# Channel mixing behind attention in a written-out order, u's parts kept in DRAM, and a sixth of its weights converted earlier

## Chip, cores, metric

One core of a Trainium2 chip runs the whole program. The metric is the device time of one execution in microseconds (us), as the median of three runs.

## What is computed

Three layers stand in a row: attention (4 batches, 8 heads, 576 positions, head size 64) as the sum of a local and a four times coarser softmax attention, a token and channel mixer, and a second mixer with a rotation.

```
x  = attention(q, k, v)                      # 4 x 576 x 512
h  = relu(x^T w_tok1) w_tok2                 # token mixing, 576 -> 256 -> 576
u  = x + h^T
x  = u + relu(u w_ch1) w_ch2                 # channel mixing, 512 -> 1536 -> 512
t  = x w_theta
y  = w_tok_r (x cos t) + w_tok_i (x sin t)   # 576 x 576
u  = x + y
out = u + relu(u w_ch)
```

All matrix products behind attention are made from a high and a low part of each operand, in three products (high x high, high x low, low x high).

## The kernel before

**Weights.** They arrive as 64-bit floats, seen as integers. A block is 128 x 256 (or 288) numbers, and `weights` (L106) converts one: a load `raw`; on ScalarE (ACT) the low word `wf` (L119) and the high word's magnitude `ww` (L121); on GpSimd (POOL), or for some of the first 33 blocks on VectorE (DVE), a clamp (L122); on DVE four operations that build the number (L126, L134) and its scale (L137, L144); on ACT the high part (L145); on POOL the difference (L146); on POOL or DVE the low part (L147). 9 blocks are of token mixing, 48 of channel mixing, 8 of `w_theta`, 18 of `w_ri`, 8 of `w_ch`.

**Channel mixing.** `channel_mix` (L184) does one batch b and one half of the 1536 channels, and in it two halves of the 576 tokens (`th`). I call one (b, half, th) a tile; there are 16. A tile loads `ut` and splits it into `uh` and `ul` (ACT and DVE, L94 and L95). Its first product runs over six blocks `cb` of 12 matmuls into a PSUM bank `c`; ACT makes the relu's high part (L214) and DVE the low part (L215), both named g in the trace. The second product runs over four blocks `db` of 18 matmuls, and DVE adds each to `ut` (L228). The result goes to `xT` in DRAM. The first half of the channels leaves u + part in `xT`, the second half splits u again, loads `xT` into `ut` and adds to it.

**Order.** A scheduler with a timeline model of its own orders the instructions of each engine from program order and priorities. In attention the string `ORDER` gives the program order: L, F, T, P, V are steps of local heads, coarse heads, token mixing and loads; `X` converts blocks of the first half's weights (24 in all), `C0` and `C1` do the first half of the channels for batches 0 and 1. Behind attention follow the first half for b = 2 and 3, then the second half for b = 0 to 3. Each tile is followed in program order by six conversions, `aside`: 24 blocks of the second half's weights, then 34 of the last layer (58 blocks over ten tiles). From there on `raw` is loaded on ACT's queue; all other loads and stores are on SP's.

Of the kernel before, what the change touches and what calls it, by code (L numbers as in the profile page):

```python
# [26 lines left out]

ORDER = """
# [3 lines left out]
T3 F5 T3 T3 L8 L8 T3 T3 P12 V10 L10 T3 T3 F5 L9 T3 T3 L9 F5 F5 L9 L9 T3 T3 P13 V11 C0 L11 L11 T4 F6 T4 F6 T4  # L32
T4 L10 L12 V12 P14 F6 T4 L10 L10 T4 T4 T4 T4 T4 F6 F6 L11 L11 T4 T4 P15 V13 L13 F7 F7 T5 T5 L12 T5 T5 L12 L12
T5 T5 V14 L14 F7 L13 L13 T5 T5 L13 F7 T5 T5 F7 T5 T5 V15 L15 C1 T6 T6 L14 L14 T6 L14 T6 T6 L15 L15 T6 L15 T6
T6 T6 T7 T7 T7 T7 T7 T7 T7 T7 T7 T6
""".split()
B, H, S, D = 4, 8, 576, 64
DM = H * D
# [21 lines left out]
def kernel(  # L60
# [23 lines left out]
    uT_d = [dram.tile([DM, S], F32, name=f"uT_{b}") for b in range(B)]  # L84
    xT_d = [dram.tile([DM, S], F32, name=f"xT_{b}") for b in range(B)]
# [18 lines left out]
    rawq = [nc.sync]  # L104

    def weights(stage, hi, lo, parts, adder=dve):  # L106

        n = hi.shape[-1]
        raw = stage.tile([128, n], parts[0][2].dtype, tag="raw", name="raw", bufs=4)
        for p0, p1, src in parts:  # L110
            rawq[0].dma_start(raw[p0:p1], src)
        if raw.dtype == I64:
            words = raw.bitcast(U32).rearrange("p (n t) -> p n t", t=2)
            high = raw.bitcast(F32).rearrange("p (n t) -> p n t", t=2)[:, :, 1]
            w = stage.tile([128, n], F32, tag="ww", name="ww")
            e = stage.tile([128, n], BF16, tag="we", name="we")
            f = stage.tile([128, n], BF16, tag="wf", name="wf")
# [6 lines left out]
            )  # L124
            wu = w.bitcast(U32)
# [10 lines left out]
            )  # L136
            dve.tensor_scalar(  # L137
# [6 lines left out]
            dve.tensor_tensor(out=f, in0=f, in1=e, op=ALU.mult)  # L144
            act.copy(hi, w)  # L145
            pool.tensor_tensor(out=w, in0=w, in1=hi.bitcast(F32), op=ALU.subtract)  # L146
            adder.tensor_tensor(out=lo, in0=w, in1=f, op=ALU.add)  # L147
        else:
            adder.tensor_copy(hi, raw)
            pool.tensor_tensor(out=lo, in0=raw, in1=hi.bitcast(F32), op=ALU.subtract)  # L150

    def load_split(pool_, stage, name, src, nk, n, chunk, adders=(pool, dve)):
# [4 lines left out]
        for c in range(0, n, chunk):  # L157
            for k in range(nk):
                def step(k=k, c=slice(c, c + chunk), adder=adders[len(steps) % len(adders)]):
                    weights(stage, hi[:, k, c], lo[:, k, c], [(0, 128, src[k * 128 : (k + 1) * 128, c])], adder)  # L160
                steps.append(step)
# [5 lines left out]
    hp = tc.alloc_tile_pool(name="hp", bufs=6)  # L167
    wlow = tc.alloc_tile_pool(name="wlow", bufs=1, side="right")
# [4 lines left out]
    def channel_weights(pool_, stage, half):  # L173
        c = slice(half * NCH, (half + 1) * NCH)
        adders = (pool, dve) if half else (pool,)
        h1, l1, s1 = load_split(pool_, stage, f"c1{half}", w_ch1[:, c], 4, NCH, 256, adders)
        h2, l2, s2 = load_split(pool_, stage, f"c2{half}", w_ch2[c, :], NCB, DM, 256, adders)
        return (h1, l1, h2, l2), s1 + s2
# [5 lines left out]
    def channel_mix(b, half, src, dst, w, mmb, queue, aside=(), per=0):  # L184

        w1h, w1l, w2h, w2l = w
        for th in range(2):
            t = slice(th * HALF, (th + 1) * HALF)
            at = f"{b}_{half}_{th}"
            here = half == 0 and b in DIRECT  # L190
# [12 lines left out]
            if half:  # L203
                queue.dma_start(ut, src[:, t].rearrange("(k p) n -> p k n", p=128))
            hs = []
            for cb in range(NCB):
                c = slice(cb * 128, (cb + 1) * 128)
# [11 lines left out]
            for db in range(4):  # L219
                d = slice(db * 128, (db + 1) * 128)  # L220
                ps = mmb.tile([128, 512], F32, tag="mb", name=f"c2_{at}_{db}")
                for cb in range(NCB):
                    pe.matmul(ps[:, 0:HALF], w2h[:, cb, d], hs[cb][0], start=(cb == 0), stop=False)  # L223
# [6 lines left out]
            for st in islice(aside, per):  # L230
                st()
# [608 lines left out]
```

## Time and profile before

| what | value |
|---|---|
| median of three runs | 787.59 us (784.44 to 788.61) |
| profiled execution: time, span | 786.98 us, 785.0 us |
| mean granted clock of TensorE | 0.959 of full speed |
| busy: TensorE (PE), DVE, ACT, POOL | 727.5, 478.5, 327.1, 263.6 us |
| moved by DMA | 91.33 MB |

The time is the device's own and holds a little work around the span. Busy time is the sum of an engine's instructions as recorded; matmuls overlap, so PE's is not its use. The clock is the share that was granted, 1.0 being 2.4 GHz and 0.5 being 1.2 GHz.

### The profile page before, as it was taken

The numbers are of one execution on the slowest core, as the hardware profiler recorded it, in microseconds if no ns is written. First come the engines' busy times: TensorE is split into PE (matmuls) and PEld (weight loads), VectorE is DVE, ScalarE is ACT, GpSimd is POOL, SyncE is SP. The second block draws the span as 40 slices with busy tenths as digits, with TensorE's granted clock in tenths as the row PEclk, the third lists the DMA queues.
The fourth block names the chain that finished last, engine by engine and source line by source line (L and its number), as shares of the span: only waits on it lengthen the run. The fifth ranks groups of instructions, "written<-read, shape, count | busy, mean of one in ns | idle before, by whom it ended". The sixth has DMA issues, their size and how long they took to land.

```text
span 785.0 us, 19821 instructions
## 1 busy us (share of the span) xinstructions
PE 727.5 (93%) x8272; PEld 684.1 (87%) x8272; DVE 478.5 (61%) x1007; ACT 327.1 (42%) x752; POOL 263.6 (34%) x276
## 2 busy tenths in 40 slices
PE   7687966899999999999898888999999999999998
PEld 4456755789988999899898888999999999999998
DVE  4998998545343332799899898423395366464432
ACT  2554645442243223455555554221384164253310
POOL 2688788422021000688788785000000000000000
PEclk9776969899999999999999999999999999999999
DMA  9566666257153213535656755231000400300101
GB/s 294 172 234 190 180 169 217 85 161 211 57 150 85 69 43 92 180 117 153 198 171 190 238 172 172 91 92 61 31 1 1 127 2 1 121 1 2 61 1 61
DMA packets 58314, 91.33 MB, mean 116 GB/s; under 512 B 7536, under 2 KB 38384, under 8 KB 58224
## 3 DMA queue, kind: packets, MB, share of 16 engines
q1 hardware_dynamic: 49872, 74.27, 30.7%
q10 hardware_dynamic: 8352, 15.80, 6.6%
q8 instruction: 65, 1.06, 0.6%
q14 instruction: 25, 0.20, 0.1%
HBM read 69.99 MB, written 20.05 MB: 115 GB/s over the span
## 4 chain that ended last, share of the span: by engine, by line
PE 56%; DVE 22%; issue 9%; POOL 6%; DMA 3%; ACT 3%; SPq 1%; ACTq 0%; POOLq 0%; DVEq 0%
PE y L98 5%; PE y L100 5%; PE y L99 5%; DVE ww L134 5%; DVE wf L144 4%; PE c L226 3%; PE c L98 3%; DVE we L137 3%; DVE ww L126 3%; PE c L223 3%; PE c L100 3%; PE c L99 3%; PE c L224 3%; POOL ww L122 3%; PE th L98 2%
## 5 line engine op out<-in xcount | busy, mean ns | idle before, releaser
L122 POOL TENSOR_SCALAR ww<-ww 128x256 f32<-128x256 f32 (+1 forms) x85 | 98.1, 1163 | 36.8 <-DVE ut L228 22.1
L215 DVE SCALAR_TENSOR_TENSOR g<-c,g 128x288 fp32r<-128x288 f32 x96 | 42.9, 450 | 62.3 <-ACT g L214 62.3
L100 PE MATMUL y<-wrh,zl 128*128 128x288 f32 x256 | 75.7, 296 | 0.0
L99 PE MATMUL y<-wrl,zh 128*128 128x288 f32 x256 | 75.6, 295 | 0.0
L98 PE MATMUL y<-wrh,zh 128*128 128x288 f32 x256 | 75.6, 296 | 0.0
L214 ACT ACTIVATE g<-c 128x288 fp32r<-128x288 f32 x96 | 38.7, 409 | 70.8 <-PE c L100 70.2
L496 POOL TENSOR_TENSOR x<-x,xu 128x640 f32<-128x640 f32 x16 | 25.3, 1591 | 106.7 <-DVE x L488 98.5
L223 PE MATMUL c<-g,c21h 128*128 128x288 f32 x192 | 53.4, 302 | 8.1 <-ACT g L214 8.1
L98 PE MATMUL c<-uh,c10h 128*128 128x288 f32 x192 | 58.2, 307 | 2.1 <-DVE ut L228 1.3
L100 PE MATMUL c<-uh,c10l 128*128 128x288 f32 x192 | 57.7, 301 | 0.0
L119 ACT ACTIVATE wf<-raw 128x256 bf16<-128x256 uint32 (+1 forms) x91 | 40.3, 443 | 41.3 <-DMA raw<-w_ch 7.8
L126 DVE TENSOR_SCALAR ww<-ww 128x256 uint32<-128x256 uint32 (+1 forms) x91 | 47.3, 521 | 16.6 <-POOL ww L122 14.8
L98 PE MATMUL c<-uh,c11h 128*128 128x288 f32 x192 | 56.9, 296 | 0.0
L99 PE MATMUL c<-ul,c10h 128*128 128x288 f32 x192 | 56.8, 296 | 0.0
L99 PE MATMUL c<-ul,c11h 128*128 128x288 f32 x192 | 56.7, 295 | 0.0
L100 PE MATMUL c<-uh,c11l 128*128 128x288 f32 x192 | 56.5, 294 | 0.0
L223 PE MATMUL c<-g,c20h 128*128 128x288 f32 x192 | 53.6, 303 | 1.6 <-ACT g L214 1.5
L224 PE MATMUL c<-g,c21l 128*128 128x288 f32 x192 | 53.1, 299 | 0.0
L224 PE MATMUL c<-g,c20l 128*128 128x288 f32 x192 | 52.2, 295 | 0.0
L134 DVE SCALAR_TENSOR_TENSOR ww<-raw,ww 128x256 uint32<-128x256 uint32 (+1 forms) x91 | 50.7, 559 | 1.0
L228 DVE TENSOR_TENSOR ut<-c,ut 128x288 f32<-128x288 f32 x56 | 25.2, 451 | 38.9 <-PE c L226 38.9
L99 PEld LDWEIGHTS y<-wrl,zh 128*128 128x128 f32 x256 | 48.1, 188 | 0.0
(190 smaller groups left out, 2274.5 us busy)
## 6 DMA issues: line engine op xcount, KB each, us to landing
qk<-qkT SPq DMA_DIRECT2D x16, 582.0 KB, 5.6
raw<-w_ch ACTq DMA_DIRECT2D x32, 256.0 KB, 2.9
ut<-uT SPq DMA_DIRECT2D x14, 576.0 KB, 4.1
xT<-ut SPq DMA_DIRECT2D x14, 576.0 KB, 3.1
vw<-vloc SPq DMA_DIRECT2D x32, 219.4 KB, 4.3
raw<-w_ch SPq DMA_DIRECT2D x24, 256.0 KB, 3.8
vd<-vtok SPq DMA_DIRECT2D x8, 650.0 KB, 6.6
raw<-w_ri ACTq DMA_DIRECT2D x18, 288.0 KB, 3.0
```

The source lines that it names most:

```text
L98: pe.matmul(out, lh, rh, start=start, stop=False)
L99: pe.matmul(out, lh, rl, start=False, stop=False)
L100: pe.matmul(out, ll, rh, start=False, stop=stop)
L119: act.activation(f, words[:, :, 0], AF.Copy, scale=2.0**-52)
L122: next(clamps).tensor_scalar(out=w, in0=w, scalar1=F64_LEAST, scalar2=F64_MOST, op0=ALU.max, op1=ALU.min)
L126: dve.tensor_scalar(out=wu, in0=wu, scalar1=3, scalar2=0x3FFFFFF8, op0=ALU.logical_shift_left, op1=ALU.bitwise_and,)
L134: dve.scalar_tensor_tensor(out=wu, in0=words[:, :, 1], scalar=0xC0000000, in1=wu, op0=ALU.bitwise_and, op1=ALU.bitwise_or)
L144: dve.tensor_tensor(out=f, in0=f, in1=e, op=ALU.mult)
L214: act.activation(h1, ps[:, 0:HALF], AF.Relu)
L215: dve.scalar_tensor_tensor(out=h2, in0=ps[:, 0:HALF], scalar=0.0, in1=h1.bitcast(F32), op0=ALU.max, op1=ALU.subtract)
L223: pe.matmul(ps[:, 0:HALF], w2h[:, cb, d], hs[cb][0], start=(cb == 0), stop=False)
L224: pe.matmul(ps[:, 0:HALF], w2l[:, cb, d], hs[cb][0], start=False, stop=False)
```

## The change

The weights of channel mixing are cut into six pieces of 256 channels instead of two halves. The fourth piece (8 blocks, named c13 and c23) is converted in attention by the new `Y` entries of `ORDER`, always with POOL for the clamp and the low part; 50 blocks stay behind attention. A conversion is now a generator (`converted`), which is advanced by half turns: load, four half turns later ACT and POOL's clamp, three later two operations of DVE, one later two more, three later ACT's high part and POOL's difference, three later the low part. A block starts at every second half turn, so some seven are under way.

Behind attention ACT, DVE, POOL and PE take program order (`manual_schedule`); SP's queue stays the scheduler's. `TURNS` gives the turns of each of the 12 tiles there, `SLOTS` the share of them that stands behind each of the ten evictions (six g, four additions). A tile's `ut` (and in the second half `uh` and `ul`) is loaded by `begin` a tile ahead; the split of the next `ut` stands, in quarters, behind the first two additions. In the first half `uh` and `ul` are stored to `parts_d`, and the second half loads them instead of splitting again. The second product takes the g of cb 0 to 3 first. `raw` stays on SP's queue.

```
-    rawq[0] = nc.scalar
+    depth[:] = 5, 6
...
-    for b in range(sum(e[0] == "C" for e in ORDER), B):
-        channel_mix(b, 0, None, xT_d[b], low, mmb if b == B - 2 else mmw, nc.sync, aside, 6)
...
+    def turn():
+        for g in list(live):
+            if next(g, "end") == "end":
+                live.remove(g)
+        g = next(blocks, lambda: None)() if next(halfturns) % 2 == 0 else None
+        if g is not None:
+            next(g)
+            live.append(g)
...
+    def begin(b, half, th):
...
+        nc.sync.dma_start(ut, src[:, t].rearrange("(k p) n -> p k n", p=128))
+        uh, ul = ((b3 if th else b1).tile([128, 4, HALF], F32R, tag=f"u{p}", name=f"u{p}_{at}") for p in "hl")
+        if half:
+            for t_, d_ in zip((uh, ul), parts_d[b][th]):
+                nc.sync.dma_start(t_.bitcast(F32), d_)
+            return (ut, uh, ul), []
+        steps = [partial(split, uh[:, kb, :], ul[:, kb, :], ut[:, kb, :]) for kb in range(4)]
+        return (ut, uh, ul), steps
...
+            for cbs in (range(4), range(4, NCB)):
+                for cb in cbs:
+                    w2h, w2l = w[cb // 2][2:4]
+                    pe.matmul(ps[:, 0:HALF], w2h[:, cb % 2, d], hs[cb][0], start=(cb == 0), stop=False)
+                    pe.matmul(ps[:, 0:HALF], w2l[:, cb % 2, d], hs[cb][0], start=False, stop=False)
+                for cb in cbs:
+                    last_one = cb == NCB - 1
+                    pe.matmul(ps[:, 0:HALF], w[cb // 2][2][:, cb % 2, d], hs[cb][1], start=False, stop=last_one)
...
+TURNS = [6, 6, 6, 5, 6, 6, 6, 6, 6, 6, 5, 0]
...
+    SLOTS = [0.08, 0.08, 0.08, 0.08, 0.02, 0.02, 0.16, 0.16, 0.16, 0.1601]
+    with tc.manual_schedule(engines={act.engine, dve.engine, pool.engine, pe.engine}):
+        loaded, steps = begin(*order[0])
...
+            def slot(i):
+                for _ in range(2 if NCB <= i < NCB + 2 else 0):
+                    next(rest, int)()
+                for _ in range(int(turns * sum(SLOTS[: i + 1])) - int(turns * sum(SLOTS[:i]))):
+                    turn()
+                next(side, int)()
+
+            mix(b, half, th, loaded, high if half else low, mmb if b == B - 2 and not half else mmw, slot)
```

In attention, DVE's queue of the kernel before reads as follows between the normalisation of a head pair (`ods`, `rl`, `x`) and the split of u (`ul`):

```order
L404 TENSOR_TENSOR ods_0_2429<-od_0_2397,rd_0_2426 128x320
L485 TENSOR_SCALAR rl_3_2484<-o_3_2443 128x10
L486 RECIPROCAL rl_3_2484<-rl_3_2484 128x10
L488 TENSOR_TENSOR x_1_2185<-o_3_2443,rl_3_2484 128x2x5x64
L215 SCALAR_TENSOR_TENSOR g_0_0_0_4_3002<-c_0_0_0_4_2988,g_0_0_0_4_3001 128x288
L215 SCALAR_TENSOR_TENSOR g_0_0_0_5_3019<-c_0_0_0_5_3005,g_0_0_0_5_3018 128x288
L95 TENSOR_TENSOR ul_0_1_3104<-um_1_1083,uh_0_1_3103 128x288 x3
```

At the same place the changed kernel has these (L136, L144, L149, L156 are the four operations of a conversion, L126, L134, L137, L144 before):

```order
L144 SCALAR_TENSOR_TENSOR ww<-raw,ww 128x256
L516 TENSOR_TENSOR x_1_2216<-o_3_2474,rl_3_2515 128x2x5x64
L149 TENSOR_SCALAR we<-ww 128x256
L136 TENSOR_SCALAR ww<-ww 128x256
L156 TENSOR_TENSOR wf<-wf,we 128x256
L144 SCALAR_TENSOR_TENSOR ww<-raw,ww 128x256
L239 SCALAR_TENSOR_TENSOR g_0_0_0_0_4_3035<-c_0_0_0_0_4_3021,g_0_0_0_0_4_3034 128x288
L149 TENSOR_SCALAR we<-ww 128x256
L156 TENSOR_TENSOR wf<-wf,we 128x256
L239 SCALAR_TENSOR_TENSOR g_0_0_0_0_5_3052<-c_0_0_0_0_5_3038,g_0_0_0_0_5_3051 128x288
L103 TENSOR_TENSOR ul_0_1_0_3137<-um_1_1114,uh_0_1_0_3136 128x288 x3
```

Conversions of the fourth piece now stand between `x`, the two g and the split; in all some 32 instructions were put between `h` of token mixing in batch 1, first half, and `h` of its second half. PE's order there stayed nearly as it was.

Behind attention, DVE's queue before has, around the end of the first product of b = 3 (g of cb 4 and 5, the next tile's split, the first addition):

```order
L215 SCALAR_TENSOR_TENSOR g_3_0_0_4_5506<-c_3_0_0_4_5492,g_3_0_0_4_5505 128x288
L137 TENSOR_SCALAR we<-ww 128x256
L147 TENSOR_TENSOR c21l<-ww,wf 128x256
L144 TENSOR_TENSOR wf<-wf,we 128x256
L215 SCALAR_TENSOR_TENSOR g_3_0_0_5_5523<-c_3_0_0_5_5509,g_3_0_0_5_5522 128x288
L126 TENSOR_SCALAR ww<-ww 128x256
L134 SCALAR_TENSOR_TENSOR ww<-raw,ww 128x256
L95 TENSOR_TENSOR ul_0_1_5700<-ut_0_1_5697,uh_0_1_5699 128x1152
L137 TENSOR_SCALAR we<-ww 128x256
L144 TENSOR_TENSOR wf<-wf,we 128x256
L126 TENSOR_SCALAR ww<-ww 128x256
L134 SCALAR_TENSOR_TENSOR ww<-raw,ww 128x256
L228 TENSOR_TENSOR ut_0_0_5418<-c_3_0_0_0_5526,ut_0_0_5418 128x288
```

and in the changed kernel:

```order
L709 SCALAR_TENSOR_TENSOR g_3_0_0_4_5683<-c_3_0_0_4_5669,g_3_0_0_4_5682 128x288
L136 TENSOR_SCALAR ww<-ww 128x256
L144 SCALAR_TENSOR_TENSOR ww<-raw,ww 128x256
L709 SCALAR_TENSOR_TENSOR g_3_0_0_5_5704<-c_3_0_0_5_5690,g_3_0_0_5_5703 128x288
L726 TENSOR_TENSOR ut_0_0_5283<-c_3_0_0_0_5707,ut_0_0_5283 128x288
L103 TENSOR_TENSOR ul_0_1_5572<-ut_0_1_5569,uh_0_1_5571 128x288 x2
L161 TENSOR_TENSOR c24l<-ww,wf 128x256
L149 TENSOR_SCALAR we<-ww 128x256
L156 TENSOR_TENSOR wf<-wf,we 128x256
L136 TENSOR_SCALAR ww<-ww 128x256
L144 SCALAR_TENSOR_TENSOR ww<-raw,ww 128x256
```

Nothing stands before the addition any more that isn't due; the conversions and two quarters of the split (x2) have moved behind it.

SP's queue of the kernel before has no `raw` behind attention; the changed one has, around the store of a finished tile (`xT`) and the loads of the next ones:

```order
L120 DMA raw<-w_ri 128x288
L688 DMA ul_1_1_6591<-ul_1_76 128x1152
L120 DMA raw<-w_ri 128x288
L688 DMA uh_1_1_6590<-uh_1_75 128x1152
L120 DMA raw<-w_ri 128x288 x3
L729 DMA xT_85<-ut_1_1_6075 128x4x288
L120 DMA raw<-w_ri 128x288
L684 DMA ut_1_1_6588<-xT_86 128x4x288
```

The loads of `ul` and `uh`, which wait for the first product of the tile that held their buffer, stand ahead of four of a tile's six raw loads.

## Rows read from the trace of the kernel before

**Rows 1.** The page, part 1: busy time, share of the span, instructions.

```profile
PE 727.5 (93%) x8272; PEld 684.1 (87%) x8272; DVE 478.5 (61%) x1007; ACT 327.1 (42%) x752; POOL 263.6 (34%) x276
```

**Rows 2.** The page, part 2: busy tenths in 40 slices; granted clock.

```profile
PE   7687966899999999999898888999999999999998
...
PEclk9776969899999999999999999999999999999999
```

**Rows 3.** Stretches: length; busy us (count) of PE, PEld, DVE, ACT, POOL; clock; DMA; GB/s.

```profile
142.39:166.79 24.40, 24.21 (x462) 21.91 (x463) 13.59 (x32) 10.52 (x28) 7.27 (x8) 0.94 0.45 134
168.00:297.00 129.00, 127.47 (x2172) 115.92 (x2172) 49.90 (x104) 39.22 (x91) 14.70 (x13) 1.00 0.35 105
296.94:558.00 261.06, 246.29 (x1812) 241.50 (x1810) 180.65 (x399) 114.53 (x276) 137.72 (x146) 0.99 0.46 143
320.00:480.00 160.00, 148.07 (x1082) 143.94 (x1081) 145.38 (x332) 87.38 (x221) 133.14 (x141) 1.00 0.56 173
500.00:558.00 58.00, 57.47 (x436) 57.24 (x434) 16.25 (x32) 11.63 (x24) 0.00 (x0) 1.00 0.22 67
```

**Rows 4.** Waits of PE from 315 to 500 us: total, times, longest us.

```profile
PE c L223 <- ACT g L214: 9.6, 10, 2.2
```

**Rows 5.** DVE groups, 320 to 480 us: busy us, mean ns, idle before.

```profile
L126 DVE TENSOR_SCALAR ww<-ww 128x256 uint32<-128x256 uint32 (+1 forms) x56 | 29.0, 518 | 7.8 <-POOL ww L122 6.4 <-DMA raw<-w_ch 1.1
L134 DVE SCALAR_TENSOR_TENSOR ww<-raw,ww 128x256 uint32<-128x256 uint32 (+1 forms) x56 | 28.2, 504 | 0.6
L144 DVE TENSOR_TENSOR wf<-wf,we 128x256 bf16<-128x256 bf16 (+1 forms) x56 | 28.0, 499 | 0.9
L137 DVE TENSOR_SCALAR we<-ww 128x256 uint16<-128x256 uint16 (+1 forms) x56 | 21.9, 391 | 0.5
L215 DVE SCALAR_TENSOR_TENSOR g<-c,g 128x288 fp32r<-128x288 f32 x43 | 19.2, 447 | 2.5 <-ACT g L214 2.5
L228 DVE TENSOR_TENSOR ut<-c,ut 128x288 f32<-128x288 f32 x30 | 13.3, 446 | 0.0
L95 DVE TENSOR_TENSOR ul<-ut,uh 128x1152 fp32r<-128x1152 f32 x7 | 9.7, 1379 | 0.0
...
L147 DVE TENSOR_TENSOR c21l<-ww,wf 128x256 fp32r<-128x256 f32 x6 | 3.7, 609 | 0.6 <-POOL ww L146 0.5
```

**Rows 6.** Groups by shape, whole span: u's split in quarters.

```profile
L95 DVE TENSOR_TENSOR ul<-um,uh 128x288 fp32r<-128x288 f32 x8 | 4.8, 618 | 0.3 <-ACT uh L94 0.3
```

**Rows 7.** The page, part 6: DMA issues, KB each, median us to landing.

```profile
raw<-w_ch ACTq DMA_DIRECT2D x32, 256.0 KB, 2.9
...
xT<-ut SPq DMA_DIRECT2D x14, 576.0 KB, 3.1
```

**Rows 8.** Two stretches of attention, columns as in rows 3.

```profile
136.00:140.00 4.00, 0.00 (x0) 0.10 (x1) 3.89 (x10) 2.33 (x8) 3.14 (x4) 0.82 0.51 208
140.00:144.00 4.00, 3.39 (x26) 2.56 (x26) 3.93 (x10) 3.13 (x10) 3.08 (x4) 0.50 0.02 4
```

**Rows 9.** Timeline of DVE: start us, length us, instruction, idle before.

```profile
110.92 0.42 DVE L134 SCALAR_TENSOR_TENSOR ww<-raw,ww 128x256 uint32<-128x256 uint32 x1
...
113.22 1.72 DVE L134 SCALAR_TENSOR_TENSOR ww<-raw,ww 128x256 uint32<-128x256 uint32 x1
...
141.97 0.42 DVE L521 SCALAR_TENSOR_TENSOR h<-t,h 128x256 fp32r<-128x256 f32 x1
...
166.79 0.42 DVE L521 SCALAR_TENSOR_TENSOR h<-t,h 128x256 fp32r<-128x256 f32 x1 [1.66 <-ACT h L520]
```

**Rows 10.** DVE groups by shape, 50 to 144.7 us.

```profile
L134 DVE SCALAR_TENSOR_TENSOR ww<-raw,ww 128x256 uint32<-128x256 uint32 x24 | 16.9, 706 | 0.2
L126 DVE TENSOR_SCALAR ww<-ww 128x256 uint32<-128x256 uint32 x24 | 13.3, 558 | 6.7 <-POOL ww L122 6.6
L144 DVE TENSOR_TENSOR wf<-wf,we 128x256 bf16<-128x256 bf16 x24 | 11.5, 485 | 0.4
L137 DVE TENSOR_SCALAR we<-ww 128x256 uint16<-128x256 uint16 x24 | 9.4, 398 | 0.2
```

More of the change, by code (lines that the diff above doesn't have):

```diff
@@ L2 @@
 from contextlib import ExitStack
-from itertools import chain, cycle, islice, repeat
+from functools import partial
+from itertools import chain, count, cycle, islice, repeat
 import numpy as np
@@ L84 @@
     uT_d = [dram.tile([DM, S], F32, name=f"uT_{b}") for b in range(B)]
+    parts_d = [
+        [[dram.tile([128, 4, HALF], F32, name=f"u{p}_{b}_{th}") for p in "hl"] for th in range(2)] for b in range(B)
+    ]
     xT_d = [dram.tile([DM, S], F32, name=f"xT_{b}") for b in range(B)]
@@ L103, with converted @@
     clamps = chain(islice(cycle([pool] * 4 + [dve]), 33), repeat(pool))
-    rawq = [nc.sync]
-    def weights(stage, hi, lo, parts, adder=dve):
+    rawq, depth = [nc.sync], [4, 3]
+    def converted(stage, hi, lo, parts, adder=dve):
         n = hi.shape[-1]
-        raw = stage.tile([128, n], parts[0][2].dtype, tag="raw", name="raw", bufs=4)
+        raw = stage.tile([128, n], parts[0][2].dtype, tag="raw", name="raw", bufs=depth[0])
         for p0, p1, src in parts:
             rawq[0].dma_start(raw[p0:p1], src)
+        yield from repeat(0, 4)
         if raw.dtype == I64:
@@ L136, in weights @@
             )
+            yield
+            e = stage.tile([128, n], BF16, tag="we", name="we", bufs=2)
             dve.tensor_scalar(
@@ L150, in weights @@
             pool.tensor_tensor(out=lo, in0=raw, in1=hi.bitcast(F32), op=ALU.subtract)
+    def weights(*args):
+        for _ in converted(*args):
+            pass
     def load_split(pool_, stage, name, src, nk, n, chunk, adders=(pool, dve)):
@@ L182, with channel_mix @@
     DIRECT = (0,)
-    def channel_mix(b, half, src, dst, w, mmb, queue, aside=(), per=0):
-        w1h, w1l, w2h, w2l = w
+    def channel_mix(b, half, src, dst, w, mmb, queue, cbs=range(NCB)):
         for th in range(2):
             t = slice(th * HALF, (th + 1) * HALF)
-            at = f"{b}_{half}_{th}"
-            here = half == 0 and b in DIRECT
+            at = f"{b}_{half}_{th}_{cbs[0]}"
+            here = src is None and b in DIRECT
             if here:
@@ new lines, with finish @@
+    live, blocks, halfturns = [], iter(highsteps), count()
+    def turn():
[6 more added lines that the diff above has]
+            live.append(g)
+    def finish():
+        while live:
+            turn()
+        assert next(blocks, None) is None
+    def begin(b, half, th):
+        at = f"{b}_{half}_{th}"
+        t = slice(th * HALF, (th + 1) * HALF)
+        ut = b2.tile([128, 4, HALF], F32, tag="ut", name=f"ut_{at}")
+        src = xT_d[b] if half else uT_d[b]
+        nc.sync.dma_start(ut, src[:, t].rearrange("(k p) n -> p k n", p=128))
+        uh, ul = ((b3 if th else b1).tile([128, 4, HALF], F32R, tag=f"u{p}", name=f"u{p}_{at}") for p in "hl")
+        if half:
+            for t_, d_ in zip((uh, ul), parts_d[b][th]):
+                nc.sync.dma_start(t_.bitcast(F32), d_)
+            return (ut, uh, ul), []
+        steps = [partial(split, uh[:, kb, :], ul[:, kb, :], ut[:, kb, :]) for kb in range(4)]
+        return (ut, uh, ul), steps
@@ L629, in stage_x @@
+    order = [(b, 0, th) for b in range(sum(e[0] == "C" and e.endswith(".3") for e in ORDER), B) for th in range(2)]
+    nlow = len(order)
+    order += [(b, 1, th) for b in range(B) for th in range(2)]
     def stage_x(b, mmp):
```

167 lines of the change are left out of this document (116 added, 51 removed).

## The prediction

> **What bounds the kernel now.** I read the totals first, then the slices, then the waits of the slices that are not full. TensorE (PE) is busy for 93% of the span [rows 1], but not evenly: each of the 40 slices is 19.6 us, and PE's nines begin only at the ninth (157 us), eights come back from the 20th to the 25th (373 to 491 us), and nines follow almost to the end [rows 2]. So there are four stretches. In 0 to 145 us PE waits for the others and its clock falls; 168 to 297 us is full (127.47 of 129 us) [rows 3]; in 297 to 500 us PE stops again and again; behind that it is full. "Busy" overstates PE, because matmuls overlap, so I count matmuls instead. From 500 to 558 us, where nothing stops it, PE starts 436 in 58.00 us, one per 0.133 us. From 296.94 us (the first matmul of the channel mixing of b = 2) to 558 us (the end of the mixing) it starts 1812 in 261.06 us [rows 3]. These need 1812 x 0.133 = 241.0 us, so **20.0 us are lost after attention**, and that is all a better order can give back there.
>
> Who takes them? The waits name g: PE stands 9.6 us in 10 pieces before the second product for ScalarE's (ACT) relu [rows 4], and shorter ones for the half of g that VectorE (DVE) makes; the rest of the 20 us I put down to the array's filling again after each stop. ACT is not full (87.38 of 160 us from 320 to 480 us); DVE is, with 145.38 of 160, 91% [rows 3]. Its work per tile (one batch's half of the tokens, half of the channels: 12 x 6 + 18 x 4 = 144 matmuls, 19.15 us) follows from its group means [rows 5]: six g at 0.447 and four additions at 0.446 make 4.47 us; the split of u 1.38 us; a converted block 0.518 + 0.504 + 0.391 + 0.499 = 1.91 us and in every second block an addition of about 0.62 us, so 2.22 us. With six blocks a tile that is 4.47 + 1.38 + 13.3 = 19.2 us against PE's 19.15. For ten tiles in a row, DVE has as much to do as PE, and what stands in front of a g in its queue decides whether PE stops.
>
> **The change part by part.**
>
> *Fewer blocks behind attention.* 58 become 50. Over the ten tiles DVE had 10 x (4.47 + 1.38) + 58 x 2.22 = 187 us to do in 191.5 us. Now the first four tiles have 4 x 4.47 + 16 x 2.22 and three splits in four pieces of 0.618 us [rows 6], 60.8 us in 76.6; the next seven have 7 x 4.47 + 34 x 2.22 = 106.8 us in 134. About 80% instead of 98%.
>
> *u's parts from DRAM.* In the second half the splits fall away (ACT and DVE, 1.38 us a tile, counted above). Loads of uh and ul take their place, each as large as a load of ut; a store of that size lands in 3.1 us [rows 7]. They are asked for a tile of 19 us ahead, so they cost nothing; without that cover it would be about 4 us a tile. The eight extra stores stand on SP behind the splits, and nobody waits for them within the tile.
>
> *The fixed order.* Turns stand behind the evictions, few at the last two g and many in the second product, and the second product takes the h of blocks 4 and 5 last. So g 5 is due 16 matmuls (2.1 us) after the first product's end. In a full tile DVE does four additions and four turns of 2.22 us behind the first of the four db (10.7 us) while PE needs three more db (7.2 us). It enters the next tile some 3.5 us late, has 6 x 0.447 and two turns (7.1 us) to do in PE's 9.6 us, and arrives in time. In the two tiles with four split pieces besides it enters 6 us late and g 5 comes about 1 us late. I take two stops of 1.2 us and some refilling: **3 us of loss remain** (bounds: 0, and 13 if the loads are late, below). The pieces of the last tiles (transposes, split of x) stay in the second to last and the last tile, their load a tile ahead. Gain here: 20 - 3 = 17 us.
>
> *Eight blocks converted during attention.* This is the price. By the order, all 32 of their DVE instructions stand between two instructions that ended at 142.39 and began at 166.79 us before (h of the token mixing, batch 1) [rows 9]. There DVE was busy 13.59 of 24.40 us [rows 3], so 10.8 us are free. What do 32 instructions cost? In the attention stretch with POOL at work the four kinds took 0.558 + 0.706 + 0.398 + 0.485 = 2.15 us a block [rows 10], together 17.2 us; at the later stretch's 1.91 us [rows 5], 15.3. Single ones differ fourfold: the same operation took 0.42 us and 1.72 us [rows 9]. POOL gets all eight clamps, subtractions and additions here, so I take the price beside a busy POOL: 13.59 + 17.2 - 24.4 = **6.4 us over**. Bounds: 0, if the instructions are the short ones (0.42 x 32 = 13.4 us would leave 2.6 us over, less what is free just ahead); and at the 91% that DVE reached at best, 30.8 / 0.91 - 24.4 = 9.4 us. The overrun is PE's: x of head pair 3 comes later, then its split, then PE's token matmuls, in whose queue nothing can pass. In 168 to 297 us only 1.5 us are free [rows 3], so it isn't made up.
>
> The Trainium skill (GPSIMD Engine Reference, section 1, Specifications) says that GpSimd's SBUF interfaces are shared with VectorE, with contention for some DVE instructions. The trace agrees as far as the 0.42 and 1.72 us go; by that rule the price beside POOL holds, by a rule without sharing it would be the short one.
>
> *No cost:* raw loads on SP instead of ACT (their issue leaves ACT, which isn't full), deeper buffers, the smaller scratch. The stretch from 558 us is the same work, and full.
>
> **Sum,** against the profiled execution's 786.98 us (0.6 us under the median of the runs): 786.98 - 20.0 + 3 + 6.4 = 776.4; with the 0.6 us, **777 us**.
>
> **The rivals.**
>
> *The cover is enough.* DVE's free 10.8 us take the eight blocks, because the short prices hold; the overrun is about 1 us. Time 786.98 - 20 + 3 + 1 = 771. For it: single short instructions. Against it: the means of both stretches.
>
> *The order doesn't free PE.* On SP four of six raw loads of a tile now stand behind the loads of ul and uh, which wait until the first product of the tile is over. Two such loads (taken as 3.1 us each) and a raw one of 2.9 us [rows 7] mean some 9 us after that point; the conversions of the third and fourth block want them some 7 us after it, and DVE, in a fixed order, would wait some 2 us a tile, in five tiles. Then 13 us of loss remain, and with the overrun it is 786.98 - 20 + 13 + 6.4 = 786.4, no change. For it: a single queue in order. Against it: a block is loaded four half turns ahead, five buffers deep.
>
> *Slower, by the clock in attention.* When PE had started nothing from 136 to 140 us its clock read 0.50 in the next 4 us [rows 8], the 1.2 GHz level; the slices below 145 us are full of this [rows 2]. If the eight blocks make PE stop so between 142 and 175 us that the whole stretch runs at 1.2 GHz, its 24.4 us of work take another 24.4 us, in place of the 6.4: 794.4. It decides, against a gain of 17 us, from about 34 us at half clock on. Against it: PE has more to do there than at 136 us, and the stops come in pieces of 1 to 4 us.
>
> The Trainium skill (TensorE: Matmul & The Clock Gate, "HAM oscillation") says that PE waits long enough between bursts put the array back to half rate, to be earned again. The trace agrees with its 0.50 behind the empty 4 us; by this rule each long stop here costs more than itself, and this rival has its chance by that.
>
> **How the numbers follow.** The forecast has 0.54, the enough cover 0.18, no freeing 0.18, the clock 0.10. Half a per cent, 3.9 us, is about what a measurement of this kernel can tell from no change: faster ends at 783.7, slower begins at 791.5. The forecast with its bounds (overrun 0 to 9.4, loss 0 to 10) spans 768 to 787; a seventh of it lies above 783.7. Faster 0.46 + 0.18 = 0.64; same 0.08 + 0.18 + 0.02 = 0.28; slower 0.08. For 8 in 10: **768 to 789 us.**
>
> **What would show it.** After attention the 1812 or so matmuls should take 244 us instead of 261, DVE about 80% busy there, hardly a PE wait for g. Between the same two instructions of attention DVE should need about 31 us instead of 24.4, and the first matmul of b = 2 should start at about 303 us instead of 296.94. If it starts before 299, the cover was enough; behind 310 with half clock ahead of it, the slower rival holds; if PE still waits for g, and DVE or ACT for raw, the order isn't what frees it.

## The result, and the profile after

The changed kernel took **776.50 us** (four runs, 776.35 to 779.66), the kernel before 787.31 us (four runs, among them the three of the table of time and profile before): ratio 0.9877, interval 0.984 to 0.9914. The prediction was 777. The profiled execution is the longest of the four, 779.66 us.

The page of the changed kernel, parts 1 and 2, against [rows 1, 2]:

```profile
PE 730.3 (94%) x8272; PEld 689.5 (89%) x8272; DVE 476.4 (61%) x1007; ACT 316.1 (41%) x756; POOL 263.9 (34%) x280
...
PE   7787966779999999999999999999999999999998
...
PEclk9775968789999999999999999999999999999999
```

A slice is 19.4 us. The eights between the 20th and the 25th slice are gone, but the eighth and ninth read 7 and 7 where they read 8 and 9. Something was gained behind attention, and something lost in it. Two rows cut the span where the two meet and where the mixing ends. The first is of PE's timeline (start us, length us); the second is of the tile `th`, the product behind the mixing (shortest, median and longest in ns, then first and last start in us):

```profile
310.94 0.29 PE L106 MATMUL c<-uh,c10h 128*128 128x288 f32 x1
```

```profile
L106 PE MATMUL th<-thh,cxh x144: 278/283/367, 550.9 to 732.6; 128*128 128x256 f32 x144
```

The mixing begins at 310.94 us (before: 296.94) and ends at 550.9 (before: 558.1). So **attention lost 14.0 us, the mixing gained 21.2**, and the span is 7.1 us shorter in this execution. A second profile of the same kernel (777.77 us) has 308.93 and 548.9: the mixing takes 240.0 us again, attention 2 us less.

Stretches of the changed kernel, columns as in [rows 3]; the first lies between the same two h of token mixing as there, from start to start:

```profile
143.31:178.82 35.51, 29.80 (x493) 26.94 (x493) 31.22 (x65) 18.94 (x53) 29.14 (x31) 0.82 0.57 179
180.00:300.00 120.00, 118.12 (x1999) 107.28 (x1999) 46.72 (x99) 38.94 (x92) 13.93 (x12) 0.97 0.43 132
310.94:550.90 239.96, 239.25 (x1812) 238.82 (x1811) 160.78 (x364) 95.03 (x253) 115.95 (x126) 1.00 0.55 181
320.00:480.00 160.00, 160.00 (x1211) 159.99 (x1210) 113.50 (x262) 65.78 (x183) 86.87 (x94) 1.00 0.63 207
```

The same 1812 matmuls take 239.96 us instead of 261.06; from 320 to 480 us PE starts 1211 instead of 1082, DVE is busy 113.5 us instead of 145.4, and no wait of PE's is left where [rows 4] stood. Between the starts of the two h, 35.51 us went by instead of 24.82 [rows 9]; DVE is busy for 88% of them and POOL for 82%, and then, from 180 us on, for 39% and 12%. DVE's timeline shows what stands in front:

```profile
160.45 0.82 DVE L516 TENSOR_TENSOR x<-o,rl 128x640 f32<-128x640 f32 x1
...
162.02 1.62 DVE L156 TENSOR_TENSOR wf<-wf,we 128x256 bf16<-128x256 bf16 x1
163.57 0.94 DVE L144 SCALAR_TENSOR_TENSOR ww<-raw,ww 128x256 uint32<-128x256 uint32 x1
...
170.81 1.68 DVE L534 TENSOR_TENSOR xl<-x,xh 128x1280 fp32r<-128x1280 f32 x1
...
178.82 0.76 DVE L549 SCALAR_TENSOR_TENSOR h<-t,h 128x256 fp32r<-128x256 f32 x2 [0.16 <-ACT h L548]
```

Conversions lie between an `x`, the split `xl` and the `h` for which PE's token mixing waits. PE's waits from 145 to 310 us show this chain (total, times, longest us), where the kernel before has none of the three:

```profile
PE c L248 <- DVE g L239: 2.3, 1, 2.3
...
PE t L106 <- ACT xh L533: 1.8, 1, 1.8
PE t L570 <- DVE h L549: 1.6, 1, 1.6
```

**Theory:** the written-out order with less work for DVE frees PE behind attention, and the eight blocks cost attention because all of them are put in front of its chain at 143 to 179 us. **Rivals:** it is the smaller load alone, or the order alone; any work added to attention costs PE what it costs DVE; attention lost for another reason.

### The profile page after: what moved, and what is told of

The parts are those of the page before. It is cut to its first block, busy times and chain, and to the rows that moved or that the text cites. A ratio compares the mean times of both kernels' runs of the same rounds, so it can differ in the third digit from the quotient of the medians.

```text
span 777.9 us, 19910 instructions
## 1 busy us (share of the span) xinstructions
PE 730.3 (94%) x8272; PEld 689.5 (89%) x8272; DVE 476.4 (61%) x1007; ACT 316.1 (41%) x756; POOL 263.9 (34%) x280
## 4 chain that ended last, share of the span: by engine, by line
PE 77%; DVE 10%; issue 4%; DMA 3%; POOL 2%; ACT 2%; SPq 1%; DVEq 0%; POOLq 0%; ACTq 0%
PE c L106 6%; PE c L108 6%; PE c L107 6%; PE y L106 5%; PE y L108 5%; PE y L107 5%; PE c L722 5%; PE c L721 5%; PE c L725 5%; PE th L106 2%; PE th L107 2%; PE th L108 2%; PE o L106 2%; PE o L108 2%; PE o L107 2%
## 5 line engine op out<-in xcount | busy, mean ns | idle before, releaser
L144 DVE SCALAR_TENSOR_TENSOR ww<-raw,ww 128x256 uint32<-128x256 uint32 (+1 forms) x91 | 52.5, 579 | 2.2
L136 DVE TENSOR_SCALAR ww<-ww 128x256 uint32<-128x256 uint32 (+1 forms) x91 | 47.6, 525 | 9.7 <-POOL ww L131 9.5
L106 PEld LDWEIGHTS y<-wrh,zh 128*128 128x128 f32 x256 | 48.1, 188 | 0.0
L108 PEld LDWEIGHTS y<-wrh,zl 128*128 128x128 f32 x256 | 48.0, 188 | 0.0
L149 DVE TENSOR_SCALAR we<-ww 128x256 uint16<-128x256 uint16 (+1 forms) x91 | 42.5, 470 | 0.4
L156 DVE TENSOR_TENSOR wf<-wf,we 128x256 bf16<-128x256 bf16 (+1 forms) x91 | 39.3, 434 | 4.0 <-DVE we L149 0.5
L106 PE MATMUL th<-thh,cxh 128*128 128x256 f32 x144 | 41.1, 285 | 0.6 <-issue 0.6
L107 PE MATMUL th<-thl,cxh 128*128 128x256 f32 x144 | 40.7, 283 | 0.0
L108 PE MATMUL th<-thh,cxl 128*128 128x256 f32 x144 | 40.7, 283 | 0.0
L130 ACT ACTIVATE ww<-raw 128x256 f32<-128x256 f32 (+1 forms) x91 | 39.5, 435 | 0.0
L107 PE MATMUL o<-cul,wch 128*128 128x288 f32 x128 | 37.4, 295 | 0.0
L108 PE MATMUL o<-cuh,wcl 128*128 128x288 f32 x128 | 37.4, 295 | 0.0
```

What stands on the lines that cost most here:

```text
L106: pe.matmul(out, lh, rh, start=start, stop=False)
L107: pe.matmul(out, lh, rl, start=False, stop=False)
L108: pe.matmul(out, ll, rh, start=False, stop=stop)
L130: act.activation(w, high, AF.Abs)
L136: dve.tensor_scalar(out=wu, in0=wu, scalar1=3, scalar2=0x3FFFFFF8, op0=ALU.logical_shift_left, op1=ALU.bitwise_and,)
L144: dve.scalar_tensor_tensor(out=wu, in0=words[:, :, 1], scalar=0xC0000000, in1=wu, op0=ALU.bitwise_and, op1=ALU.bitwise_or)
```

## The experiments

Each kernel is the changed one with one edit, or the one with the late blocks (second below) with one edit; later mixing and the last kernel have two. Each ratio is against runs of the kernel before made in the same series, so it is not the quotient of the medians shown. The two times in the right half are those of the two rows above, in each kernel's own profile. A profile is one execution, so these times have some play: that of order alone (790.57 us) is 4.5 us above its median, that of the changed kernel 3.2 us, of late, split again 2.8 us.

| kernel | median us | ratio to before (interval) | mixing begins | ends | takes |
|---|---|---|---|---|---|
| before | 787.31 | | 296.94 | 558.1 | 261.2 |
| changed | 776.50 | 0.9877 (0.984 to 0.9914) | 310.94 | 550.9 | 240.0 |
| changed again | 777.46 | 0.9865 (0.9847 to 0.9883) | 308.93 | 548.9 | 240.0 |
| no blocks | 769.70 | 0.9769 (0.974 to 0.9798) | 299.63 | 539.6 | 240.0 |
| late blocks | 770.35 | 0.9774 (0.9745 to 0.9804) | 302.40 | 542.4 | 240.0 |
| scheduler's order | 791.89 | 1.005 (1.0033 to 1.0067) | 309.71 | 565.0 | 255.3 |
| order alone | 786.05 | 0.9992 (0.9969 to 1.0015) | 303.25 | 561.8 | 258.6 |
| late, split again | 777.87 | 0.9902 (0.9867 to 0.9937) | 311.28 | 551.7 | 240.4 |
| late, burst | 822.69 | 1.0461 (1.0423 to 1.0499) | 300.29 | 591.1 | 290.8 |
| late, product order | 772.77 | 0.9831 (0.9793 to 0.987) | 300.81 | 541.7 | 240.9 |
| late, raw on ACT | 778.03 | 0.9892 (0.9856 to 0.9929) | 302.67 | 549.6 | 246.9 |
| late third piece | 786.18 | 0.9982 (0.9961 to 1.0003) | 318.08 | 558.3 | 240.2 |
| later mixing | 780.47 | 0.9913 (0.9889 to 0.9938) | 311.03 | 551.0 | 240.0 |
| no blocks, no parts | 767.37 | 0.9763 (0.9738 to 0.9787) | 297.54 | 538.1 | 240.6 |

Attention is the same program in late blocks, burst, product order and raw on ACT, and its end lies between 300.29 and 302.67 us: profiles differ by some 2 us there.

**No blocks.**

```
-        first_iter = iter(firststeps)
+        first_iter = iter(first)
...
-                for st in islice(first_iter, int(e[1:])):
-                    for _ in st():
-                        pass
+                t_ = next(first_iter).rearrange("p k (a n) -> p (k a) n", n=128)
+                act.copy(t_, id16.unsqueeze(1).to_broadcast([128, 8, 128]))
```

> The changed kernel without the conversion of the eight blocks of the fourth piece in attention: four ScalarE copies of 128 x 1024 elements fill the piece with copies of an identity matrix instead, so channel mixing with that piece computes something else. Theory A (the eight blocks are what delays attention by 14.0 us, the first matmul of b = 2 at 310.94 us instead of 296.94): that matmul comes back to 297 us (295 to 299), the time falls by 12 to 15 us to 762 to 765 us. Rival (the delay comes from something else in attention, the weights in six pieces, the other order or the clock): the first matmul of b = 2 stays behind 306 us and the time at 774 to 778 us.

The blocks are the main cause: without them the mixing begins at 299.63 us. The time fell less than expected, to 769.7. The ratios of the changed kernel's two series lie 0.0096 and 0.0108 above this one's, 7.6 to 8.5 us: that is the blocks' price, and the intervals leave some 3 us of play on either side. Some 2.7 us of the 14.0 belong to something else (last experiment).

**Late blocks.** Eight entries `Y1.p` in place of four `Y2`, further back in `ORDER`:

```
...
+                n, p = (int(i) for i in e[1:].split("."))
+                with tc.issue_after(exps[pairs[p]].ins):
+                    for st in islice(first_iter, n):
```

> The changed kernel with the same eight blocks converted later in attention, one at a time, each behind the softmax exponential of a later head pair (10 to 14), in 190 to 300 us, where VectorE was 30 to 45% and GpSimd 8 to 15% busy. Theory A (the price is that eight blocks stand in a bunch ahead of the instructions for which TensorE's token mixing waits, not what they cost as such): the 143 to 179 us stretch returns to some 25 us between the two h, the first matmul of b = 2 starts at 297 to 301 us, the time is 762 to 768 us, 8 to 14 us below the changed kernel and below both kernels. Rival (32 more VectorE instructions and 24 of GpSimd cost TensorE as much wherever they stand in attention, since attention is a chain through all engines): first matmul of b = 2 at 307 us or later, time 773 to 779 us.

Its stretches, columns as above, and its four kinds of conversion instructions from 178 to 262 us (busy us, mean ns, idle before):

```profile
140.00:180.00 40.00, 38.59 (x722) 33.18 (x726) 20.27 (x43) 17.41 (x46) 12.69 (x13) 0.89 0.63 196
180.00:260.00 80.00, 76.81 (x1513) 69.36 (x1506) 45.01 (x106) 33.46 (x84) 32.46 (x33) 1.00 0.47 148
```

```profile
L144 DVE SCALAR_TENSOR_TENSOR ww<-raw,ww 128x256 uint32<-128x256 uint32 x8 | 4.4, 555 | 0.1
...
L156 DVE TENSOR_TENSOR wf<-wf,we 128x256 bf16<-128x256 bf16 x8 | 4.0, 512 | 0.0
...
L136 DVE TENSOR_SCALAR ww<-ww 128x256 uint32<-128x256 uint32 x8 | 2.9, 361 | 11.2 <-POOL ww L131 11.2
L149 DVE TENSOR_SCALAR we<-ww 128x256 uint16<-128x256 uint16 x8 | 2.7, 344 | 0.1
```

All eight blocks are converted, and the time is that of the kernel without them (770.35 and 769.70, ratios 0.9774 and 0.9769). From 140 to 180 us PE is busy 38.59 us. DVE even stands 11.2 us for POOL's clamps, and the time shows nothing of it. So the price was not the work; **it was the place** ahead of PE's chain, in a bunch. This run moved the blocks and spread them at once, so it doesn't say what either does alone. By its median this is the fastest complete version, and it is clear of the changed kernel: its interval ends at 0.9804, that of the changed kernel's second series begins at 0.9847.

**Scheduler's order.**

```
-    with tc.manual_schedule(engines={act.engine, dve.engine, pool.engine, pe.engine}):
+    with ExitStack():
```

The evictions get back the high priority that they had before:

```
-            act.activation(h1, ps[:, 0:HALF], AF.Relu)
...
+            with tc.high_priority(offset=2000):
+                act.activation(h1, ps[:, 0:HALF], AF.Relu)
...
```

> The changed kernel with the written-out order of ScalarE, VectorE, GpSimd and TensorE behind attention given back to the scheduler, with the evictions (g and the additions) at high priority as in the kernel before; the program order, the eight blocks in attention and the parts in DRAM stay. Theory (the order is what frees TensorE): its stops for g return, 8 to 16 us of the 21 gained between the first matmul of b = 2 and the end of the mixing are lost again, time 784 to 792 us. Rival (the load frees it: 50 blocks instead of 58 and no second split leave VectorE at 80%, and any order does): mixing stays within 3 us of 240 us, time 774 to 780 us.

PE's waits from 309 to 565 us (total, times, longest):

```profile
PE c L722 <- ACT g L709: 3.3, 3, 1.8
PE c L106 <- DVE g L710: 2.0, 2, 1.4
PE c L726 <- DVE g L710: 1.8, 3, 0.9
```

The waits for g are back, 15.3 of the 21.2 us are gone again, and with attention's loss this kernel is slower than before. So the smaller load gives 5.9 us in the order that this scheduler makes of the new program. The three waits are 7.1 of the 15.3 us; PE's busy time for the same matmuls is 7.6 us longer too (246.87 instead of 239.25), and no run here shows why.

**Order alone.** Blocks of the fourth piece are converted behind attention again:

```
...
-TURNS = [6, 6, 6, 5, 6, 6, 6, 6, 6, 6, 5, 0]
+TURNS = [8, 8, 8, 7, 6, 6, 6, 6, 6, 6, 5, 0]
...
-    high, highsteps = [first], []
+    first, highsteps = channel_weights(whigh, stg, 3)
+    high = [first]
```

> The changed kernel with the eight blocks converted behind attention again, 24 in the first four tiles (turns 8, 8, 8, 7): the written-out order and the parts in DRAM without the earlier conversion. Theory A (attention pays 14 us for the blocks, the order is worth more than the blocks): attention as in the kernel before, first matmul of b = 2 at 297 us; in the first four tiles VectorE has 24 x 2.22 + 4 x 4.47 + 3 x 2.47 = 78.6 us to do in 76.6, so 2 to 8 us are lost there; time 765 to 772 us, below the changed kernel. Rival (the earlier conversion is needed to free VectorE): TensorE waits for g or for VectorE's additions in the first four tiles for 14 us or more, time 777 us or more.

Stretches, and a wait of ACT's and one of DVE's from 303 to 400 us:

```profile
303.25:341.00 37.75, 31.20 (x220) 30.53 (x218) 12.87 (x30) 13.76 (x36) 9.75 (x11) 0.91 0.36 121
341.00:400.00 59.00, 53.40 (x376) 51.43 (x377) 53.22 (x126) 28.44 (x83) 46.05 (x54) 0.97 0.69 232
400.00:561.80 161.80, 161.22 (x1218) 161.00 (x1218) 109.05 (x243) 60.42 (x159) 80.36 (x87) 1.00 0.51 168
```

```profile
ACT wf L128 <- DMA raw<-w_ch: 7.7, 2, 5.2
```

```profile
DVE g L708 <- ACT g L707: 15.4, 5, 12.2
```

At 0.1324 us a matmul (239.96 / 1812) the first stretch loses 37.75 - 220 x 0.1324 = 8.6 us, the second 59 - 49.8 = 9.2, the third nothing. My 78.6 us of DVE's work in 76.6 left out the start: until 341 us DVE is busy a third of the time. The waits say why: the first raw blocks are late, ACT waits for them in its fixed order, and DVE in its own for ACT's relu. From 341 to 400 us DVE is busy for 90%. So the order needs the earlier conversion as much as that needs the order: alone they give 2.6 us (in the profile that is 4.5 us above its median) and 5.9, together 21.2.

**Late, split again.** The parts in DRAM undone:

```
...
-        if half:
-            for t_, d_ in zip((uh, ul), parts_d[b][th]):
-                nc.sync.dma_start(t_.bitcast(F32), d_)
-            return (ut, uh, ul), []
...
```

> The kernel with the late blocks, with the parts in DRAM undone: nothing is stored to the parts, the second half of the channels loads u a tile ahead, splits it again in quarters behind the first two additions, and then loads the first half's result over it. Theory A (the parts save VectorE what makes a full tile fit): a tile with six blocks has 4.47 + 2.2 + 13.3 = 20.0 us for VectorE against TensorE's 19.15, so 3 to 8 us are lost in the five tiles that have six; attention keeps its time: 773 to 778 us. Rival B (the splits fit, and the stores of the parts in attention, up to now taken for free, are what attention lost beside the eight blocks, some 3.6 us): mixing stays at 240 us, first matmul of b = 2 some 3 us earlier than the 302.40 us of the late blocks, time 766 to 768 us. Neither: 769 to 772 us.

Neither theory's time. The mixing takes 240.4 us, so DVE has room for the splits. Attention takes 8.9 us longer than in late blocks, though it has less to do. Wait of PE, and stretch, both 240 to 260 us:

```profile
PE t L567 <- DVE h L546: 3.6, 1, 3.6
```

```profile
240.00:260.00 20.00, 16.43 (x253) 13.68 (x252) 7.27 (x20) 7.94 (x23) 5.72 (x7) 0.74 0.17 48
```

Without the eight stores the scheduler ordered attention in another way (of DVE's 423 instructions there, 366 keep their order). PE stands 3.6 us for an h, and its clock reads 0.74 over these 20 us.

**Late, burst.** `SLOTS = [0, 0, 0, 0, 0, 0, 0, 0, 0, 1.0001]`: all turns behind the last addition.

> The kernel with the late blocks, with all turns of a tile behind its last addition instead of spread over the ten evictions (the same instructions per tile in another place of each engine's order). Theory (where the steps stand between the evictions is what keeps TensorE going): 13 us of VectorE's conversions stand in a row ahead of the next tile's first g, TensorE has banks for six blocks (9.6 us) before it must wait, so each of the eleven tiles with turns loses 3 to 8 us: mixing 270 to 320 us instead of 240.0, time 800 to 850 us. Rival (any fixed order will do as long as VectorE has room in a tile): mixing within 5 us of 240, time 769 to 776 us.

The wait that comes of it, from 300 to 595 us:

```profile
PE c L723 <- DVE g L711: 27.6, 6, 5.4
```

50.8 us are lost with the same instructions, 35.5 us more than in the scheduler's order: without the spreading a fixed order is worse than none. The wait shown is 27.6 of them; PE's clock reads 0.93 over this mixing, where it read 1.00.

**Late, product order.** `for cbs in (range(NCB),):` in the second product.

> The kernel with the late blocks, with the second product's order of the kernel before: all high parts of the six blocks first, then the six low parts, instead of blocks 0 to 3 first. The high part of block 5 is then due 10 matmuls (1.3 us) behind the first product's end instead of 14 (1.9 us), the low part of block 0 no earlier than before. Theory (ScalarE and VectorE now have little in front of the last two g, so 1.3 us is enough for most): mixing 240 to 244 us, time within 4 us of the late blocks' 770.35. Rival (the waits of the kernel before, 9.6 us in 10 pieces for ScalarE's g, came from this order): 0.5 to 1 us in each of 12 tiles, mixing 246 to 252 us, time 776 to 782 us.

0.9 us in the mixing, and the two intervals overlap: this part of the change does nothing that can be measured.

**Late, raw on ACT.** `rawq[0] = nc.scalar` behind attention.

> The kernel with the late blocks, with the raw loads behind attention asked for by ScalarE's queue instead of SP's, as in the kernel before. In the changed kernel ScalarE waited 12.8 us in all for raw blocks without TensorE's losing time. Theory (the loads come early enough on either queue, and TensorE has no wait to be removed): mixing 239 to 242 us, time within 2 us of 770.35. Rival (an issue on ScalarE that waits for a free raw buffer holds back the g behind it in a fixed order): each such wait of 1 to 4 us stops TensorE, mixing 245 us or more, time 775 us or more.

ACT's timeline at the seam, and PE's one wait in the mixing:

```profile
320.69 0.38 ACTq L120 DMA_DIRECT2D raw<-w_ch  x1
321.11 0.41 ACT L711 ACTIVATE g<-c 128x288 fp32r<-128x288 f32 x1 [2.70 <-issue]
```

```profile
PE c L106 <- DVE g L712: 4.9, 1, 4.9
```

The rival was right, but once, not in each tile: at the end of attention the issue of a raw load stands in front of the first tile's third g. In late blocks, too, the first raw load goes out some 19 us behind the mixing's begin (321.84 us), but there it stands on SP's queue, and that g starts at 311.07 us. The stop and PE's slow start behind it cost 6.9 us; the stretch behind the stop reads 0.69 of the clock:

```profile
320.00:330.00 10.00, 7.93 (x46) 7.93 (x47) 1.98 (x5) 3.75 (x12) 0.76 (x1) 0.69 0.31 100
```

**Changed again.** No edit.

> The changed kernel once more, on the same chip as the two that follow. Its profiled execution was the longest of its four (779.66 us, the others 776.35 to 776.65), with the first matmul of b = 2 at 310.94 us. If the extra 3 us stood in attention, as the 11.3 us between that and the kernel without the blocks (299.63 us) against 6.8 us between the medians (776.5 and 769.7) suggest, this profile shows that matmul at 306 to 309 us and the mixing again at 240 us; if they stood elsewhere, it is at 310 to 312 us again.

308.93 us: the 1.9 us between the two profiled executions lie in attention.

**Late third piece, later mixing.** The last eight of the 24 blocks for the first half of the channels behind later head pairs; in the second kernel the mixing of b = 0 later too. Of the first kernel's edit to `ORDER`, the places where the blocks move (the lines are cut short):

```
-P9 T2 L6 F3 V7 X S
+P9 T2 L6 F3 V7 X4 S
...
-V11 C0.0.3 L11
+V11 X2.8 X3.9 X3.10 C0.0.3 L11
```

> The kernel with the late blocks, with the last eight of the 24 blocks of the first half also converted later: behind the exponentials of head pairs 8, 9 and 10 instead of pair 1; channel mixing of b = 0 stays where it was in program order. Theory A (VectorE's and GpSimd's time ahead of 145 us is what costs, since VectorE is 69.6 of 80 us busy from 60 to 140 us and TensorE stands 24 us there, and behind 145 us it is nearly free): 8 x 2.15 = 17 us of VectorE leave the tight stretch, attention goes ahead faster there, a third to all of it reaches the end: 754 to 765 us. Rival B (the blocks are needed early, because the channel mixing of b = 0 is what TensorE fills its stops with): TensorE stands for the third piece instead, 767 to 774 us. Rival C (the eight blocks again stand in a bunch, now at 155 to 200 us): 775 us or more.

> As the kernel before in this list, with the channel mixing of b = 0 also put later in the program order (behind the load of head pair 14) and two blocks each behind the exponentials of pairs 8 to 11. Theory A: the third piece is due later still, so no bunch at 190 us, 752 to 764 us. Rival B (the mixing of b = 0 is TensorE's filler, and later it has none): 3 to 10 us over the kernel before in this list.

Theory A fell in both. Stretches of the first, and two of PE's waits there from 60 to 300 us:

```profile
120.00:140.00 20.00, 19.46 (x299) 16.21 (x283) 7.09 (x16) 6.67 (x19) 2.88 (x2) 0.86 0.50 148
180.00:200.00 20.00, 15.46 (x150) 13.98 (x149) 16.54 (x35) 11.00 (x28) 17.22 (x18) 0.74 0.62 190
```

```profile
PE c L106 <- ACT c12h L158: 2.1, 1, 2.1
...
PE c L108 <- POOL c12l L161: 1.4, 1, 1.4
```

Attention did go ahead: the exponential of head pair 8 starts at 139.35 us instead of 152.78. But the mixing of b = 0 could not fill PE's stops without its third piece, the blocks stood in a bunch at 180 to 200 us, and more was given back than gained: from 140 to 200 us PE is busy 45.9 of 60 us, in late blocks 58.6. The mixing of b = 2 begins at 318.08 us instead of 302.40, and at 311.03 in the second kernel, whose third piece is waited for longer (3.7 us for its low parts). Which of the two rivals, the missing filler or the bunch, weighs more is not shown.

**No blocks, no parts.** The edits of no blocks and of split again together; DVE's order in attention is that of the kernel before.

> The kernel without the eight blocks (the same ScalarE copies fill the piece, so channel mixing with it computes something else), with the parts in DRAM undone as well: nothing is stored to them, the second half splits u again in quarters. In attention VectorE's order is then, instruction by instruction, that of the kernel before, while without the stores alone it was not; the written-out order behind attention stays. Open is why attention took some 3.6 us longer than before even without the blocks (299.63 us against 296.94 at the first matmul of b = 2, and 17.5 us between the medians where the mixing alone gained 21.1). Theory A (the eight stores in attention, and the other order that the scheduler makes with them there): the first matmul of b = 2 returns to 296 to 298 us, the mixing stays at 240 to 241 us, the time is 3 to 4 us under that of the kernel without the blocks, 765 to 767 us. Rival B (something else in attention, as the copies or the pools): first matmul at 299 to 301 us, time 769 to 771 us.

The mixing begins at 297.54 us, as before the change, with 2.1 us less than without the blocks alone. Between the medians it is 2.3 us, between the ratios only 0.5: the profiles show the mechanism, the times don't resolve its size. The waits of PE from 145 to 297 us have only one left, that of the kernel before; with the stores (no blocks) there were also these:

```profile
PE t L107 <- DVE xl L534: 1.3, 2, 1.0
PE od L418 <- ACT us L582: 1.0, 1, 1.0
```

## Why the prediction came out, point by point

**What can be given back: right.** 20.0 us were counted from matmuls, 21.2 were gained. That the part of it beyond the waits was the array's filling again is a supposition that no run tests.

**What remains: 3 us, measured 0.** The step that failed is that DVE enters a tile late, with two stops of 1.2 us. PE has no wait from 315 to 500 us; even with a split in every tile (240.4 us) it has none. The block came out as counted: 0.541 + 0.528 + 0.476 + 0.350 = 1.90 us and half an addition of some 0.62, 2.21 us against 2.22. What was wrong is to add durations up, because the records of successive DVE instructions overlap: from 320 to 480 us they add up to 125.2 us, and DVE is busy 113.5. So the 98% counted for the kernel before was 91% in the profile [rows 3], and 440 to 460 us of the changed kernel, in the thick of the conversions, have 87%. With nine tenths of the counted durations (an estimate from 113.5 / 125.2), DVE enters a tile with split pieces 4.7 us late instead of 6 and is done 11.2 us into it, before g 5 is due at 11.7. (Such tiles are three, not two.) Neither the smaller load nor the order did this alone (255.3 and 258.6 us). The stretch and the means in the changed kernel, the latter from 320 to 480 us:

```profile
440.00:460.00 20.00, 20.00 (x153) 20.00 (x152) 17.46 (x38) 9.86 (x27) 15.65 (x17) 1.00 0.80 269
```

```profile
L144 DVE SCALAR_TENSOR_TENSOR ww<-raw,ww 128x256 uint32<-128x256 uint32 (+1 forms) x38 | 20.6, 541 | 1.3
L149 DVE TENSOR_SCALAR we<-ww 128x256 uint16<-128x256 uint16 (+1 forms) x38 | 20.1, 528 | 0.0
L136 DVE TENSOR_SCALAR ww<-ww 128x256 uint32<-128x256 uint32 (+1 forms) x38 | 18.1, 476 | 0.0
...
L156 DVE TENSOR_TENSOR wf<-wf,we 128x256 bf16<-128x256 bf16 (+1 forms) x37 | 13.0, 350 | 2.4 <-DVE we L149 0.5
```

**The eight blocks: 6.4 us, measured 7.6 to 8.5** (10.7 between the two h in the profile, above my bound of 9.4). With some 3 us of play the times don't exclude 6.4; the profiles are further off, with a first matmul of b = 2 at 310.94 and 308.93 us where 303 was forecast. The place was right, and DVE's work too: 31.2 us busy where 30.8 were summed, four kinds at 0.650 + 0.586 + 0.557 + 0.385 = 2.18 us where I took 2.15. What I left out is that DVE stands between two of them: 35.51 - 31.22 = 4.3 us, 1.9 of it for POOL's clamps, which are part of the same blocks. And I took the overrun as the price of the work; late blocks shows that it is the price of its place. What part of the 10.7 us is the clock's is not separated: PE stands 5.7 of the 35.51 us, and its clock reads 0.82 where it read 0.94.

```profile
L144 DVE SCALAR_TENSOR_TENSOR ww<-raw,ww 128x256 uint32<-128x256 uint32 x9 | 5.8, 650 | 0.1
L136 DVE TENSOR_SCALAR ww<-ww 128x256 uint32<-128x256 uint32 x9 | 5.3, 586 | 1.9 <-POOL ww L131 1.9
L156 DVE TENSOR_TENSOR wf<-wf,we 128x256 bf16<-128x256 bf16 x9 | 5.0, 557 | 0.4
L149 DVE TENSOR_SCALAR we<-ww 128x256 uint16<-128x256 uint16 x9 | 3.5, 385 | 0.1
```

The Trainium skill's rule that GpSimd shares SBUF interfaces with VectorE (GPSIMD Engine Reference, section 1, Specifications) goes with this: a block took 2.18 us where POOL was busy 29.14 of 35.51 us, and 0.555 + 0.512 + 0.361 + 0.344 = 1.77 us in late blocks, where it was 32.46 of 80. But POOL's being busy is not what sets the price: the 0.42 us of [rows 9] stood beside a busy POOL as well as the 1.72 (last section).

**Edits costed at nothing.** The loads of the parts cost the mixing nothing and also save it only 0.4 to 0.6 us; their stores cost attention about 2 us in the profiles of the kernels without blocks. Whether that is the other order or the stores' own traffic is not separated, and with the late blocks it was the kernel without the stores whose attention took longer, by 8.9 us. Raw loads on SP cost nothing, but that sentence missed what they are worth: 6.9 us in a fixed order.

**The sum.** -21.2 + 8.0 (the middle of the blocks' price) + 2.1 makes 776.2 us from 787.31. That the total fitted to half a microsecond is luck: the freeing was taken 4 us too small and attention's loss about 4 us too small, and the two errors cancel.

**The rivals.** Enough cover: not where the blocks were put; where cover is, its 771 us came true (770.35). Order that doesn't free PE, for late raw loads: no wait of PE's shows it, though ACT did wait 4.4 us for raw in the mixing. The clock in attention: it did fall, to 0.82 between the two h, and the mixing began behind 310 us in one profile of two, but far from the 34 us at half clock that this rival needs.

## What to carry to other kernels

Work moved under an engine's idle time costs by what stands behind it in that engine's queue: look for the chain's next instructions, and put the work in small pieces behind events that come late enough, not in a bunch at the first place with some room. An engine's load is read from its busy time; durations added up count what overlaps twice. An order written by hand and the load that it has to carry are one decision; try each alone before you credit either. Work that fills another engine's stops is not free to move, however idle it looks.

## What the runs showed of the hardware beyond that

The same DVE instruction differs several times over: in the changed kernel's timeline `wf<-wf,we` takes 0.29 us in one place and 1.62 us at 162 us. By the trace, what decides is which instruction POOL runs beside it. POOL's timeline beside the 0.42 and the 1.72 us of [rows 9] in the kernel before, and beside the 1.62 us:

```profile
110.29 2.13 POOL L122 TENSOR_SCALAR ww<-ww 128x256 f32<-128x256 f32 x2
...
113.12 3.25 POOL L496 TENSOR_TENSOR x<-x,xu 128x640 f32<-128x640 f32 x2
```

```profile
161.91 1.58 POOL L524 TENSOR_TENSOR x<-x,xu 128x640 f32<-128x640 f32 x1
```

The short one stands beside clamps, which have one operand; the long ones begin inside an addition of two operands and end 0.15 us or so after one. Counted over the changed kernel's trace, the four kinds (128x256) take 0.28, 0.42, 0.28 and 0.29 us (L136, L144, L149, L156) where POOL does nothing, 76 instructions with no more than 0.02 us above that. Of 95 that begin inside a two-operand instruction of POOL, 88 end 0.15 to 0.29 us after the end of that one. All 80 that take over 0.3 us longer stand beside such a one; clamps alone add at most 0.25 us. So the price of a block is set by POOL's two-operand work beside it, not by POOL's busy share.

A short stop of PE's costs more than itself: with a wait of 4.9 us up to 322.07 us in raw on ACT, the clock of the 10 us from 320 was 0.69, and 6.9 us were gone. The Trainium skill (TensorE: Matmul & The Clock Gate, "HAM oscillation") says that waits between bursts make PE start cold again, and this row agrees.

Open stays why the scheduler's other order of attention (split again, at 311.28 us) comes out so much worse than the one with the stores; a single wait of 3.6 us and the clock behind it are what the profile shows of 8.9 us.
